# The first heads of a fused attention, routing and feed-forward kernel: small GpSimd transfers moved back, zeros on TensorE, one head prepared a step later

## The chip, the cores and the metric

The kernel runs on 1 core of one Trainium2 chip. The metric is the device time of one execution in microseconds (us). Before the change it is 897.05 us, the median of 3 runs (896.64 to 898.61). The changed kernel is timed in the same way.

The core has TensorE (PE in the profile; its weight loads are PEld), VectorE (DVE), ScalarE (ACT), GpSimd (POOL) and SyncE (SP). SP and POOL issue the transfers (DMA) of this kernel, each from a queue of its own that is worked off in order.

## The reference, cut to what matters

Three stages follow each other. Only the first is touched by the change.

```python
scores = scale * np.matmul(q, k.transpose(0, 1, 3, 2))      # 4 x 8 heads, 576 rows, 64 wide
cum = np.cumsum(np.maximum(s, 0.0), axis=-1)
bias = -(cum[:, :, :, None] - cum[:, :, None, :])
scores = np.where(causal, -1e9, scores + np.minimum(bias, 0.0))
attn = softmax(scores)                                      # with 1e-9 in the sum
x = np.matmul(attn, v)                                      # heads side by side: 2304 x 512
x = moe(x, w_gate, w1, w2)          # each token goes to one of 8 experts, 288 tokens each
out = gelu_like(x @ w_in) @ w_out   # h / (1 + exp(-1.702 h)) between the two products
```

## The kernel before, in words

**Heads and steps.** The 32 heads of attention run as a software pipeline. One step of the list `SEQ` works on several heads at once: in step i, TensorE computes the scores of head i+1 (`S`, in three units 2, 1, 0), transposes the probabilities of heads i and i-1 (`T`) and multiplies older ones with v (`A`); VectorE does row maxima (`M`) and the low parts (`L`); ScalarE does the exponentials (`X`) and the high parts (`H`). In the order of a step, `S2` of the next head comes early, then `T3` and `A0` of the head before, then `S1`, `T0`, `T1`, `A1`, `S0`. The score tiles have few buffers: `S2` of a head reuses the buffer that `X2` of the head before has read.

**Preparing a head.** For each head, q and k are written as a high and a low part into two stacked operands, `X0[i]` (first 128 rows of the contraction) and `X1[i]` (68 rows). `X1` is one tile `x1` with `HS = 6` slots. Its rows 64 to 67 hold ones, minus ones and the running sums of s: first ones and minus ones are put there for all slots, then each head's sums are written over half of them by two transfers of 4.5 KB from the DRAM tile `c_rows` (`part("c", i)`, L110 and L111). `scores` issues for each unit the products with `X0` (x = 0) and then those with `X1` (x = 1).

- Heads 0 and 1 are prepared by ScalarE and VectorE (L113 to L121), with loads per head (L310) and their sums written straight from SBUF (L327, L328).
- Heads 2 and 3: ScalarE does three operations (`Aq` L113, `Ak` L115, `Aq1` L117), GpSimd two (`kl` L106, `ql` L104).
- Heads from 4 on: ScalarE does one (`Aq`), GpSimd three (`k` L102, `kl`, `ql`), and SP copies q's high part (`q1`, L108, a transfer of 145 KB).

`load(j)` (L79) brings q and k of the pair of heads 2j and 2j+1 in four transfers of 290 KB; `load_v(j)` (L85) brings v of a pair in two (280 and 10 KB); `split_v` (L91, L92, on GpSimd) makes its high and low parts.

**What sets the order.** The first block, from the first load to `load(3)`, is ordered by hand on all five queues: SP and POOL issue there in the order of the text. From the steps on only PE, ACT and DVE are ordered by hand; the order on SP and POOL comes from the planner. `HIGH` tells in which step `high(i)` of a head is issued: `HIGH.get(j, j - 5)`. For heads from 4 on `prep(i)` (v, the sums' transfers, `k`, `kl`) goes at the head of that same step. An odd head's `high` also issues the next load, `load((i + 5) // 2)`, which needs the buffer of the pair two before it.

**GpSimd's transfers at the start.** `rest` (L318) copies the ones and minus ones of slot 0 to slots 1 to 5: 4 partitions, issued at once after the constants. Two more (L341) bring the gate's weights into `fold`, in pieces of 32 bytes.

**Zeros on TensorE.** Later in the kernel, `pulse` (L691) multiplies a tile of zeros to keep TensorE busy between the routing's small products. Before the change nothing of the kind stands at the start.

Of the kernel before, what the change touches and what calls it, by code (L numbers as in the profile page):

```python
# [8 lines left out]
F32 = mybir.dt.float32  # L9
# [9 lines left out]
BF = mybir.dt.bfloat16  # L19
# [9 lines left out]
P, T = 116, 5  # L29
# [13 lines left out]
def f32(ap):  # L43
    return ap.bitcast(F32)
# [3 lines left out]
def tile_kernel(ctx, tc, qt, kt, v, s, w_gate, w1, w2, w_in, w_out, out):  # L48
    nc = tc.nc
    V, A, G, PE, SY = nc.vector, nc.scalar, nc.gpsimd, nc.tensor, nc.sync  # L50
    keep = ctx.enter_context(tc.tile_pool(name="keep", bufs=1))
# [10 lines left out]
    ps = actx.enter_context(tc.tile_pool(name="ps", bufs=2, space=PSUM))  # L62
# [4 lines left out]
    st = {}  # L67
# [5 lines left out]
    def load(j):  # L73

        b, h = divmod(2 * j, H)
        t = att.tile([128, 2, 2, SP], F32, name="raw", bufs=3)
        for n, src in enumerate((qt, kt)):
            for r in (slice(0, 64), slice(64, 128)):
                SY.dma_start(t[r, n], src[b, h:h + 2].rearrange("h d s -> d h s"))  # L79
        st["raw", j] = t  # L80

    def load_v(j):
        t = att.tile([P, 2, T, D], F32, name="vraw", bufs=3)
        for r in (slice(0, 112), slice(112, P)):
            SY.dma_start(t[r].rearrange("p g t d -> p (g t d)"), v[j, r])  # L85
        st["v", j] = t
# [12 lines left out]
    def part(what, i):  # L99
        t, x0, x1 = st["raw", i // 2][:, :, i % 2], X0[i % HS], X1[i % HS]  # L100
        if what == "k":
            return G.tensor_scalar(x0[:, 1], t[:, 1], sc[:, 1:2], None, op0=OP.mult)  # L102
        if what == "ql":
            return G.tensor_tensor(x0[UP, 0], t[UP, 0], f32(x0[UP, 0]), op=OP.subtract)  # L104
        if what == "kl":
            return G.tensor_tensor(x1[LO, 1], t[LO, 1], f32(x0[LO, 1]), op=OP.subtract)  # L106
        if what == "q1":
            return SY.dma_start(f32(x1[LO, 0]), f32(x0[LO, 0]))  # L108
        if what == "c":
            SY.dma_start(f32(x1[66:68, 0]), c_rows[i])  # L110
            return SY.dma_start(f32(x1[64:66, 1]), c_rows[i])  # L111
        if what == "Aq":
            return A.activation(x0[:, 0], t[:, 0], AF.Copy, scale=sc[:, 0:1])  # L113
        if what == "Ak":
            return A.activation(x0[:, 1], t[:, 1], AF.Copy, scale=sc[:, 1:2])  # L115
        if what == "Aq1":
            return A.activation(x1[LO, 0], t[LO, 0], AF.Copy, scale=0.125)  # L117
        if what == "Vql":
            return V.tensor_tensor(x0[UP, 0], t[UP, 0], f32(x0[UP, 0]), op=OP.subtract)
        if what == "Vkl":  # L120
            return V.tensor_tensor(x1[LO, 1], t[LO, 1], f32(x0[LO, 1]), op=OP.subtract)  # L121

    def prep(i, c=True):
        if i % 2 == 0 and i // 2 + 1 < NH // 2:
            load_v(i // 2 + 1)
        if c:
            part("c", i)
        if i >= 4:
            part("k", i)
            part("kl", i)  # L130
        if i % 2 == 0:
            split_v(i // 2 - 1)
        elif i == NH - 1:
            split_v(i // 2)

    def high(i):

        if 2 <= i < 4:
            for what in ("Aq", "Ak", "Aq1"):
                part(what, i)  # L140
            part("kl", i)
        elif i >= 4:
            part("Aq", i)
            part("q1", i)
        if i >= 2:
            st["prep", i] = part("ql", i)
        if i % 2 and (i + 5) // 2 < NH // 2:
            load((i + 5) // 2)
# [8 lines left out]
    def scores(i, u, xs=(0, 1), mask=True):  # L157
        X = X0[i % HS], X1[i % HS][:68]
        if ("sc", i, u) not in st:
            st["sc", i, u] = ps.tile([P, 1024 if u == 0 else 512], F32, name="s4" if u == 0 else "sc", bufs=1 if u == 0 else 2)  # L160
        p = st["sc", i, u]
        banks = [c0 // 512 for _, c0, _, _ in UNITS[u]]
        for m, (t, c0, k0, w) in enumerate(UNITS[u]):
            for x in xs:
                PE.matmul(p[:, c0:c0 + w], X[x][:, 0, t * P:(t + 1) * P], X[x][:, 1, k0:k0 + w],  # L165
                          start=x == 0 and banks[m] not in banks[:m],
                          stop=x == 1 and (k0 + w < (t + 1) * P if mask else banks[m] not in banks[m + 1:]))
        if not mask:
            return
        d, n = DIAG[u], len(DIAG[u])  # L170
        step = d[-1] - d[0] if n > 1 else P
        o = p[:, d[0]:d[0] + n * step].rearrange("p (a c) -> p a c", a=n)[:, :, :P] if d[0] + n * step <= p.shape[1] \
            else p[:, d[0] + P - step:d[0] + P - step + n * step].rearrange("p (a c) -> p a c", a=n)[:, :, step - P:]
        PE.matmul(o, identb[:P, :P], maskb[:P, None, :P].to_broadcast([P, n, P]), start=False, stop=1 in xs)  # L174
# [113 lines left out]
    x1 = consts.tile([128, HS, 2, SP], F32R, name="x1")  # L288
# [10 lines left out]
    wg = w_gate.rearrange("(h d) e -> d h e", d=D)  # L299
    sums = consts.tile([P, 5, T, 2], F32, name="sums")  # L300
    warm = consts.tile([1, 2], F32, name="warm")
    G.memset(warm, 0.0)
    with (tc.manual_schedule(engines={PE.engine, A.engine, V.engine, SY.engine, G.engine})):

        SY.dma_start(cs, s)
        first_raw = st["raw", 0] = att.tile([128, 2, 2, SP], F32, name="raw", bufs=3)
        for i in range(2):
            for n, src in ((0, qt), (1, kt)):
                for r in (LO, UP):
                    SY.dma_start(first_raw[r, n, i], src[0, i])  # L310
        A.activation(warm, warm, AF.Exp)
        G.memset(f32(x1[64:68, 0, 0]), 1.0)
        V.memset(f32(x1[64:68, 0, 1]), -1.0)
        G.memset(sc, 1.0)
        G.memset(sc[LO, 0:1], 0.125)
        G.memset(sc[UP, 1:2], 0.125)
        rest = f32(x1[64:68, 1:]).rearrange("p i n s -> p i (n s)")
        G.dma_start(rest, f32(x1[64:68, 0]).rearrange("p n s -> p (n s)")[:, None, :].to_broadcast(list(rest.shape)))  # L318
        G.memset(sums, 1e-9)

        V.tensor_scalar(cs, cs, 0.0, None, op0=OP.max)
        V.tensor_tensor_scan(c_sum, cs, cs, 0.0, op0=OP.add, op1=OP.max)
        A.activation(chl[:, 0], c_sum, AF.Copy)
        V.tensor_scalar(identf, jp, 0.0, None, op0=OP.is_equal)
        V.tensor_tensor(chl[:, 1], c_sum, f32(chl[:, 0]), op=OP.subtract)
        for h in range(2):
            SY.dma_start(f32(X1[h][66:68, 0]), f32(chl[h:h + 1]))  # L327
            SY.dma_start(f32(X1[h][64:66, 1]), f32(chl[h:h + 1]))  # L328
        SY.dma_start(c_rows, f32(chl))
        for what in ("Aq", "Ak", "Aq1", "Vql", "Vkl"):  # L330
            part(what, 0)
        V.tensor_scalar(identb, jp, 0.0, None, op0=OP.is_equal)
        V.tensor_scalar(maskb, jp, 0.0, -1e9, op0=OP.is_gt, op1=OP.mult)
        for what in ("Aq", "Ak", "Aq1", "Vql", "Vkl"):
            st["prep", 1] = part(what, 1)
        V.tensor_tensor(fold[:, :, :D], identf[:, None, :D].to_broadcast([128, H, D]),
                        identf[:, None, D:].to_broadcast([128, H, D]), op=OP.add)
        load(1)
        load_v(0)
        for g in range(2):  # L340
            G.dma_start(fold[g * D:(g + 1) * D, :, D:], wg)  # L341
        part("c", 2)
        prep(3)
        load(2)
        load_v(1)
        prep(2, False)
        load(3)

    FN = dict(S=lambda i, u: scores(i, u) if i else scores(0, u, (1,), False), M=row_max, X=exps, T=transp, H=p_hi, L=p_lo, A=av, O=av_out, N=norm, R=recip, F=fin, G=fin_out)

    HIGH = {2: 0, 3: 0, 4: 1, 5: 1, 6: 2, 7: 2}

    def steps(i0, i1):
        for i in range(i0, i1):
            new = [j for j in range(NH) if HIGH.get(j, j - 5) == i]
            for j in new:
                if j >= 4:
                    prep(j)
            for f, lag, *a in SEQ:
                if f == "Q":  # L360
                    for j in new:
                        high(j)
                else:
                    on(FN[f], i - lag, *a)
# [2 lines left out]
    att_engines.enter_context(tc.manual_schedule(engines={PE.engine, A.engine, V.engine}))  # L367
    for u in (2, 1, 0):
        scores(0, u, (0,))
    steps(-3, 14)  # L370

    zeros = keep.tile([128, 128], BF, name="zeros")
    late = ExitStack()
    late.enter_context(tc.issue_after(st["prep", 17].ins))
    G.memset(zeros, 0.0)
    jrow = rt.tile([128, 128], F32, name="jrow")
    G.iota(jrow, pattern=[[1, 128]], base=0, channel_multiplier=0, allow_small_or_imprecise_dtypes=True)
    pcol = rt.tile([128, 1], F32, name="pcol")
# [782 lines left out]
    with tc.manual_schedule(engines={PE.engine, A.engine, V.engine}):  # L1161
        for q in range(NQ):
            c, p = divmod(q, PP)
# [54 lines left out]
            n, src = (4, g[:, :4]) if last else (7, g[:, 1:])  # L1218
# [52 lines left out]
```

## Time and profile before

| | |
|---|---|
| median of 3 runs | 897.05 us (896.64 to 898.61) |
| profiled execution, its own time | 896.56 us |
| span of that execution, first to last instruction | 894.8 us |
| what lies around the span | 1.76 us |
| mean granted TensorE clock | 0.973 of full speed |
| PE busy | 840.4 us, 94% of the span, 6853 matmuls |
| DVE, ACT, POOL busy | 723.6, 509.0, 276.8 us |
| moved by DMA | 124.38 MB |
| PE's busy tenths in the first five of 40 slices | 4, 7, 9, 9, 9 |

The page cuts the span in 40 slices of 22.4 us. In the first two, PE is busy for less than 8 tenths, in the following ones for 9 and more. Everything that the change edits is issued in the first 60 us. A busy PE need not be at full speed: the granted clock of a stretch says which of two levels, 1.2 and 2.4 GHz, it had (0.50 and 1.00 in the profile). Where a wait is for several things, the profile names the one that came last by its own account.

### The profile page before, as it was taken

Reading aid. Unit: us, or ns where it says so; the run is one execution under the profiler, and the core shown is the slowest. Engines: PE = TensorE matmul, PEld = TensorE weight load, DVE = VectorE, ACT = ScalarE, POOL = GpSimd, SP = SyncE. Lnnn points to the kernel's source line nnn. Section 1 sums busy time; section 2 is a strip of 40 time slices with the busy share of each in tenths; the row PEclk is TensorE's granted clock in tenths of the full one; section 3 lists DMA queues with packets and bytes.
Section 4 is the critical chain, followed back from the end, with each engine's and each line's share of the span. In section 5 each row is a group of like instructions: output and inputs, shape, how many; then the busy total and the mean of one; then the engine's idle time right before and its main releaser. Section 6 shows DMA issues by size and latency. Waiting matters only on the chain.

```text
span 894.8 us, 18574 instructions
## 1 busy us (share of the span) xinstructions
PE 840.4 (94%) x6853; PEld 821.0 (92%) x6853; DVE 723.6 (81%) x1683; ACT 509.0 (57%) x1141; POOL 276.8 (31%) x263
## 2 busy tenths in 40 slices
PE   4799999999669899999999999999999999999996
PEld 3699999999538899999999999999999999999996
DVE  4678889888777689999897798899978977777775
ACT  5889998997534557666664343434335434444442
POOL 2999999983242111021100011111010111111112
PEclk9899999999769999999999999999999999999999
DMA  6886558620346689888874333323256111111101
GB/s 160 193 199 167 149 136 217 156 75 6 123 146 104 226 243 280 258 270 248 258 236 181 99 118 101 118 83 111 73 189 222 56 49 48 48 48 49 48 24 49
DMA packets 88391, 124.38 MB, mean 139 GB/s; under 512 B 10541, under 2 KB 56769, under 8 KB 87781
## 3 DMA queue, kind: packets, MB, share of 16 engines
q1 hardware_dynamic: 85156, 113.55, 43.4%
q0 software_dynamic: 3136, 9.57, 3.7%
q8 instruction: 57, 0.93, 0.4%
q14 instruction: 42, 0.34, 0.1%
HBM read 96.61 MB, written 22.21 MB: 133 GB/s over the span
## 4 chain that ended last, share of the span: by engine, by line
PE 48%; DVE 12%; issue 4%; ACT 3%; DMA 2%; POOL 1%; SPq 0%; POOLq 0%; DVEq 0%; ACTq 0%
PE h L1013 13%; PE y L1045 11%; PE y L908 11%; PE h L898 11%; DVE g L1031 3%; DVE gT L1223 3%; ACT gT L1219 2%; DVE g L1025 2%; DVE part L1076 1%; PE h L873 1%; DVE tmp L1076 1%; DMA wi_dram<-wist 1%; DVE u L814 1%; DMA raw<-in_moe_w_in_dram 1%; DVE yc L941 1%
## 5 line engine op out<-in xcount | busy, mean ns | idle before, releaser
L1013 PE MATMUL h<-yc,win 128*128 128x256 f32 x1728 | 218.6, 283 | 0.0
L1013 PEld LDWEIGHTS h<-yc,win 128*128 128x128 f32 x1728 | 212.4, 192 | 0.0
L1045 PE MATMUL y<-wout,gT 128*128 128x256 f32 x1491 | 189.6, 282 | 7.0 <-DVE part L1076 3.9
L1045 PEld LDWEIGHTS y<-wout,gT 128*128 128x128 f32 x1491 | 180.9, 189 | 9.7 <-issue 4.2
L1219 ACT ACTIVATE gT<-g 128x896 fp32r<-128x896 f32 x72 | 68.4, 950 | 140.5 <-DVE g L1031 139.6
L908 PE MATMUL y<-hT,w2s 128*128 128x288 f32 x768 | 115.8, 299 | 0.0
L898 PE MATMUL h<-xT,w1s 128*128 128x288 f32 (+2 forms) x776 | 114.2, 295 | 0.0
L908 PEld LDWEIGHTS y<-hT,w2s 128*128 128x128 f32 x768 | 107.4, 191 | 0.0
L898 PEld LDWEIGHTS h<-xT,w1s 128*128 128x128 f32 x776 | 106.5, 188 | 0.1
L217 DVE TENSOR_TENSOR phl<-pt,phl 116x464 fp32r<-116x464 f32 (+1 forms) x128 | 76.2, 599 | 28.0 <-ACT phl L212 27.9
L1223 DVE TENSOR_TENSOR gT<-g,gT 128x896 fp32r<-128x896 f32 x72 | 78.9, 1096 | 16.4 <-ACT gT L1219 16.3
L1031 DVE TENSOR_TENSOR g<-g 128x128 f32<-128x128 f32 x284 | 75.2, 306 | 4.9
L228 PE MATMUL pt<-phl,vhl 116*128 116x232 f32 (+2 forms) x512 | 75.7, 291 | 2.4 <-POOL vhl L92 2.1
L212 ACT ACTIVATE phl<-pt 116x464 fp32r<-116x464 f32 (+1 forms) x128 | 69.2, 541 | 12.4 <-PE pt L206 12.1
L670 POOL DMA_INDIRECT xg<-x_rows,idx x24 | 29.3, 1222 | 141.2 <-PE h L873 134.8
L228 PEld LDWEIGHTS pt<-phl,vhl 116*128 116x128 f32 x512 | 66.4, 194 | 4.0 <-POOL vhl L92 2.8
L1080 POOL DMA_INDIRECT out_dram<-part,oids x18 | 22.2, 1231 | 150.5 <-DVE part L1076 150.5
L1020 ACT ACTIVATE sg<-h 128x256 f32<-128x256 f32 x84 | 32.1, 384 | 64.1 <-PE h L1013 63.5
L206 PE MATMUL pt<-identf,pr 116*116 116x116 f32 x480 | 66.7, 271 | 0.9 <-DVE phl L217 0.7
L1021 DVE TENSOR_TENSOR g<-h,sg 128x256 f32<-128x256 f32 x84 | 35.5, 423 | 32.9 <-ACT sg L1020 32.3
L165 PE MATMUL sc<-x 128*116 128x348 f32 (+3 forms) x192 | 44.8, 342 | 16.0 <-ACT x L115 10.4
L206 PEld LDWEIGHTS pt<-identf,pr 116*116 116x116 f32 x480 | 52.5, 143 | 4.4 <-PE sc L174 1.0
(199 smaller groups left out, 1433.6 us busy)
## 6 DMA issues: line engine op xcount, KB each, us to landing
wraw<-in_moe_w_dram SPq DMA_DIRECT2D x60, 512.0 KB
yraw<-y_dram SPq DMA_DIRECT2D x18, 512.0 KB
raw<-in_qt_dram SPq DMA_DIRECT2D x30, 290.0 KB
raw<-in_kt_dram SPq DMA_DIRECT2D x30, 290.0 KB
raw<-in_moe_w_in_dram SPq DMA_DIRECT2D x32, 256.0 KB
raw<-in_moe_w_out_dram SPq DMA_DIRECT2D x32, 256.0 KB
y_dram<-yt SPq DMA_DIRECT2D x8, 576.0 KB
vraw<-in_v_dram SPq DMA_DIRECT2D x16, 280.0 KB
```

What stands on the lines that cost most here:

```text
L165: PE.matmul(p[:, c0:c0 + w], X[x][:, 0, t * P:(t + 1) * P], X[x][:, 1, k0:k0 + w], start=x == 0 and banks[m] not in banks[:m], stop=x == 1 ...
L206: PE.transpose(p[:, w - P:w], pr[:, place(t, c):place(t, c + 1)], identf[:P, :P])
L212: A.activation(hl[:, 0], p, AF.Copy)
L217: st["lo", i] = V.tensor_tensor(hl[:, 1], st["pt", i, g], f32(hl[:, 0]), op=OP.subtract)
L228: PE.matmul(p[:, t0 * P:(t0 + n) * P], vhl[:, hh, c].rearrange("p a d -> p (a d)"), st["phl", i, g][:, x, col:col + n * P], start=x == 0 a ...
L898: PE.matmul(p[:, o], w[:, a, k, c], x[:, b, k, o], start=n == 0 and (e, m) != (0, 0), stop=n == len(steps) - 1)
L908: PE.matmul(py[d], w[:, a, m % 2, d * 128:(d + 1) * 128], h[:, b], start=m == 0 and n == 0, stop=m == 7 and n == 2)
L1013: PE.matmul(h, w[:, a, k], yc[c][:, b, k], start=n == 0 and (both is None or half == 0), stop=n == 11 and (both is None or half == 1))
L1031: V.tensor_tensor(g[:, o], g[:, a], g[:, b], op=op)
L1045: PE.matmul(acc[b][:, o * 256:o * 256 + 256], t[:, j, x], wout[:, p, i, y], start=p == 0 and n == 0 and b not in banks[:m], stop=end and n ...
L1219: A.activation(t[:, 0, :n], src, AF.Copy)
L1223: V.tensor_tensor(t[:, 1, :n], src, f32(t[:, 0, :n]), op=OP.subtract)
```

## The change

- `rest` moves from the constants to behind `load_v(0)`. In front of it POOL now does a `tensor_copy` of one number out of v's first tile, and a `memset` that sets that number's place back. `rest` covers slots 2 to 5 only; the two memsets of slot 0 (L312, L313) now cover slots 0 and 1. The two `fold` transfers stay behind it.
- `idle(n)` is new: n products of zeros, 128 x 512, into a PSUM tile of the transposes' kind. `idle(12)` is PE's first work; `idle(6)` comes after the x = 0 products of head 0's scores and before the x = 1 products. The tile `zeros` is made at the start instead of later.
- `HIGH` puts heads 3, 5 and 7 one step later each: 3 in step 1, 5 in step 2, 7 in step 3. With them go their loads, `load(4)`, `load(5)` and `load(6)`, and for 5 and 7 the work of `prep`.

```diff
+    zeros = keep.tile([128, 128], BF, name="zeros")
+    G.memset(zeros, 0.0)
     G.memset(warm, 0.0)
+    def idle(n):
+        p = ps.tile([P, 512], F32, name="pt", bufs=4)
+        for i in range(n):
+            PE.matmul(p, zeros[:, :P], zeros[:, None, :].to_broadcast([128, 4, 128]), start=i == 0, stop=i == n - 1)
...
         A.activation(warm, warm, AF.Exp)
-        G.memset(f32(x1[64:68, 0, 0]), 1.0)
-        V.memset(f32(x1[64:68, 0, 1]), -1.0)
+        idle(12)
+        G.memset(f32(x1[64:68, 0:2, 0]), 1.0)
+        V.memset(f32(x1[64:68, 0:2, 1]), -1.0)
...
-        rest = f32(x1[64:68, 1:]).rearrange("p i n s -> p i (n s)")
-        G.dma_start(rest, f32(x1[64:68, 0]).rearrange("p n s -> p (n s)")[:, None, :].to_broadcast(list(rest.shape)))
...
         load(1)
         load_v(0)
+        G.tensor_copy(sums[:1, 0, 0, 1:2], st["v", 0][:1, 1, 0, :1])
+        G.memset(sums[:1, 0, 0, 1:2], 1e-9)
+        rest = f32(x1[64:68, 2:]).rearrange("p i n s -> p i (n s)")
+        G.dma_start(rest, f32(x1[64:68, 0]).rearrange("p n s -> p (n s)")[:, None, :].to_broadcast(list(rest.shape)))
         for g in range(2):
             G.dma_start(fold[g * D:(g + 1) * D, :, D:], wg)
         part("c", 2)
...
-    HIGH = {2: 0, 3: 0, 4: 1, 5: 1, 6: 2, 7: 2}
+    HIGH = {2: 0, 3: 1, 4: 1, 5: 2, 6: 2, 7: 3}
...
     for u in (2, 1, 0):
         scores(0, u, (0,))
+    idle(6)
     steps(-3, 14)
-    zeros = keep.tile([128, 128], BF, name="zeros")
     late = ExitStack()
     late.enter_context(tc.issue_after(st["prep", 17].ins))
-    G.memset(zeros, 0.0)
```

## Rows read from the trace of the kernel before

**Rows 1.** TensorE's instructions in order of time: first scores of steps 1 to 5.

```profile
24.06 0.71 PE L165 MATMUL sc<-x 128*116 128x348 f32 x4 [2.53 <-POOL x L106]
...
27.67 1.79 PE L228 MATMUL pt<-phl,vhl 116*128 116x348 f32 x6 [2.13 <-POOL vhl L92]
...
33.87 0.71 PE L165 MATMUL sc<-x 128*116 128x348 f32 x4
...
40.14 0.39 PE L165 MATMUL sc<-x 128*116 128x348 f32 x1
42.89 0.55 PE L165 MATMUL sc<-x 68*116 68x348 f32 x3 [2.36 <-DMA x<-c_rows]
...
50.94 0.72 PE L165 MATMUL sc<-x 128*116 128x348 f32 x4
...
57.22 0.71 PE L165 MATMUL sc<-x 128*116 128x348 f32 x4
```

**Rows 2.** Busy time by stretch: us, length, PE, PEld, DVE, ACT, POOL, clock, DMA share, GB/s.

```profile
6.00:7.00 1.00, 0.00 (x0) 0.00 (x0) 0.76 (x1) 0.00 (x0) 0.00 (x0) 1.00 0.28 35
...
25.00:31.00 6.00, 3.87 (x17) 3.26 (x16) 4.18 (x11) 4.74 (x14) 6.00 (x4) 0.50 1.04 214
32.00:45.00 13.00, 10.58 (x94) 10.04 (x94) 8.72 (x21) 9.81 (x29) 12.82 (x10) 1.00 0.79 169
...
46.00:48.00 2.00, 2.00 (x11) 1.75 (x10) 0.63 (x2) 0.92 (x5) 1.92 (x3) 0.50 0.51 121
...
50.00:60.00 10.00, 10.00 (x92) 9.89 (x91) 8.39 (x23) 9.16 (x27) 9.85 (x8) 1.00 0.97 234
```

**Rows 3.** ScalarE in order of time: preparing heads 0, 2 and 3.

```profile
9.56 0.78 ACT L115 ACTIVATE x<-raw,sc 128x580 fp32r<-128x580 f32 x1 [3.69 <-DMA raw<-in_kt_dram]
...
19.83 0.78 ACT L115 ACTIVATE x<-raw,sc 128x580 fp32r<-128x580 f32 x1 [1.79 <-DMA raw<-in_kt_dram]
...
21.09 0.76 ACT L113 ACTIVATE x<-raw,sc 128x580 fp32r<-128x580 f32 x1
...
23.00 0.53 ACT L192 ACTIVATE pr<-sc,nm 116x348 f32<-116x348 f32 x1
```

**Rows 4.** SP's queue in order of time: issues of transfers, neighbours merged.

```profile
2.44 1.24 SPq L310 DMA_DIRECT2D raw<-in_kt_dram  x2
3.71 3.85 SPq L310 DMA_DIRECT2D raw<-in_qt_dram  x2
...
9.06 0.74 SPq L327 DMA_DIRECT2D x<-xs  x1
...
12.14 1.41 SPq L79 DMA_DIRECT2D raw<-in_qt_dram  x2
...
18.47 1.89 SPq L79 DMA_DIRECT2D raw<-in_qt_dram  x2
...
33.57 0.23 SPq L110 DMA_DIRECT2D x<-c_rows  x1
...
38.80 2.55 SPq L108 DMA_DIRECT2D x<-x  x2
```

**Rows 5.** GpSimd in order of time: rest's issue, v's cast, two low parts.

```profile
2.22 0.98 POOL L318 DMA_DIRECT2D x<-x  x1
...
21.05 0.72 POOL L91 CAST vhl<-vraw 116x640 fp32r<-116x640 f32 x1 [1.46 <-DMA vraw<-in_v_dram]
...
38.82 2.79 POOL L106 TENSOR_TENSOR x<-raw,x 64x580 fp32r<-64x580 f32 x2
```

**Rows 6.** DMA issues of the first 60 us: KB each, median us to landing.

```profile
x<-x POOLq DMA_DIRECT2D x1, 90.6 KB, 6.7
```

**Rows 7.** The chain that ended last, at the routing's gather: start, us.

```profile
266.59 3.72 DMA xg<-x_rows,idx
```

**Rows 8.** VectorE in order of time: its wait for the first load.

```profile
2.64 0.45 DVE L321 TENSOR_SCALAR xs<-xs 32x580 f32<-32x580 f32 x1 [1.19 <-DMA xs<-in_s_dram]
```

**Rows 9.** TensorE in order of time: zeros of the routing, after idle time.

```profile
259.60 3.19 PE L691 MATMUL warm<-zeros 128*128 128x512 bf16 x7
```

## The prediction

> **What bounds the kernel now.** Read first the page's busy shares in 40 slices: PE is short of work in the first two slices and near the end of attention, nearly nowhere else, and all that the change edits is issued in the first 60 us. So the question is what the first steps cost. Read second PE's own order of time and look only at where each step's first scores stand [rows 1]. From 50.94 to 57.22 a step takes 6.28 us with PE busy throughout [rows 1, 2]; that is the price of a step that lacks nothing. Step 1 (24.06 to 33.87) takes 9.81, step 2 (33.87 to 40.14) 6.27, step 3 (40.14 to 50.94) 10.80. Step 1 has lost 3.5 us and step 3 4.5. From step 4 on PE is full until the routing, so a shift of step 4's start, now at 50.94, should reach the end one for one. I forecast that one number.
>
> Third, the clock of these stretches [rows 2]: 0.50 from 25 to 31 and from 46 to 48, that is 1.2 GHz of 2.4. Each follows an idle PE by some us: the wait in front of 24.06 (2.53) and the one in front of 42.89 (2.36) [rows 1]. A wait of this length costs itself and then some us at the lower level.
>
> Fourth, who ends the waits. In step 0, ScalarE stands until 19.83 for k of heads 2 and 3 [rows 3], then does two operations for head 2 and three for head 3, and only at 23.00 the exponential that frees the buffer for the scores of 24.06; the profile names GpSimd, which came about as late. In step 1, PE waits 2.13 for v's low part [rows 1], since v's cast could only begin at 21.05, when v had landed [rows 5]. In step 3 it waits for a transfer into x. The queue shows which: the copy of q's high part for head 4 is issued at 38.80 [rows 4], behind two more loads of pairs, with issues that stand for earlier transfers to land from 33.57 on.
>
> **Part 1: GpSimd's transfers leave the start.** rest is issued at 2.22 [rows 5] and needs 6.7 us to land [rows 6]. Meanwhile the DMA engines are at 0.28 (6 to 7 us) though ScalarE waits until 9.56 for k of head 0 [rows 2, 3]: about 4.5 of 16 engines work, which fits 4 partitions of rest on a few engines that all loads need too. SP is held as well: two issues take 3.85 us where the two before took 1.24 [rows 4]. With rest and fold gone I expect each issue at 0.62. SP's 8 loads then end at 2.44 + 6 x 0.62 = 6.2 instead of 8.85, and the rest of its list moves forward by 2.6 to 2.9: load(1) from 12.14 to 9.3 [rows 4]. Taking 2.9: k of heads 2 and 3 lands at 16.9 instead of 19.83, v at 18.1 instead of 21.05 [rows 3, 5]. Bounds: 0 if the stall was not rest's, 3.5 if the loads also land faster.
>
> **Part 2: they come back behind v.** GpSimd now stands until v has landed (18.1); the copy and the memset take some 0.2 (between nothing and the cast's 0.72 [rows 5]); then it issues rest. When rest lands is not in the trace. The bounds: 6.7, rest's own time among the loads [rows 6], and 1.9, the first load of s (issued at 0.72, used at 2.64 [rows 8]). The nearest row is a GpSimd transfer on an otherwise quiet DMA, the routing's gather, 3.72 [rows 7], and SP will be quiet here. I take it: rest lands at 18.3 + 3.7 = 22.0.
>
> The Trainium skill ("DMA: Bandwidth & Descriptors", section on the anatomy of one SWDGE transfer) fits a transfer issued by GpSimd as 2.0 us plus its bytes over 436 GB/s; for these 74 KB that is an estimate of 2.2, and by it all that follows would come 1.5 us sooner. The two rows on GpSimd's transfers here, 3.72 and 6.7, are both above it, so it is not used.
>
> Behind that landing two queues stand. On SP the sums of head 2 (c) write into rows that rest writes, so they wait, and behind them the sums of head 3, load(2), v of the next two pairs and load(3). On GpSimd, fold's two issues (1.46 by the row of before, which is not on the path), the cast, and head 2's low part wait for v; they are through at about 23, before PE asks. The sums are issued at 22.0 and 22.3 (0.23 each [rows 4]) and take the 1.9 of a small load to land: PE gets the x = 1 scores of head 2 at 24.2, against 24.06 before. So step 0 gains nothing: what part 1 saves is spent on waiting for rest. ScalarE is through with head 2 by 19.4 and idles.
>
> **Part 3: zeros.** One product of zeros takes 3.19 / 7 = 0.46 us at the lower clock [rows 9], half of that at the upper. idle(12) takes at most 5.5 us from 1.3 on and ends at about 6.8, when k of head 0 has come: hidden. idle(6) puts 1.4 to 2.7 us in front of head 0's x = 1 products; its cover is the wait for rest, since ScalarE's exponentials of head 1 would end at 19.4 and PE waits until 24.2. Without that cover the 1.4 to 2.7 would be on the path. What the zeros give: a higher clock for heads 0 and 1, which then wait anyway. PE idles for about 5 us before 24.2, twice the idles that preceded the lower clock, so step 1 begins at 1.2 GHz as before. I cost part 3 at 0.
>
> **Part 4: head 3 a step later.** Three ScalarE operations (21.09 to 23.00, 1.91 us [rows 3]) leave step 0 and enter step 1, head 5's one leaves step 1 for step 2, and so on; by step 3 the sum is the same. GpSimd's two operations for head 3 move too, and load(4), load(5), load(6).
>
> *Step 1.* Gone: the wait for v's low part, 2.13. Added on ScalarE: 1.91 less the one operation of head 5 (0.76); but the exponentials of head 1, which stood in step 1 before, are done while PE waits for rest. I take 9.81 - 2.13 + 0.3 = 8.0, between 6.28 (nothing lost) and 9.81. Step 2 begins at 32.2 and step 3 at 38.5 (6.27, as before).
>
> *Step 3.* It needs c and q1 of head 4. Before, load(4) stood ahead of them on SP; now load(4) belongs to step 1 and needs the buffer of heads 2 and 3, which GpSimd frees late, so I expect q1 ahead of it. What is still ahead: load(2), load(3) and three loads of v, 3.2 MB. Before, v's arrival at 21.05 freed the DMA engines for load(2) and q1 landed at 42.86, with 4.4 MB in between: 203 GB/s. Now load(2) is issued at 23.1, behind four transfers of sums, and data flow some 1.5 later: 24.6 + 3.2 MB / 203 = 40.4. PE waits 1.9 us instead of 2.36 and scores head 4 at 40.4 instead of 42.89.
>
> *To step 4.* Before, 42.89 to 50.94 is 8.05; with a clock that holds it is 6.28 - 0.39 = 5.9. The wait of 1.9 is shorter than both that were followed by the lower clock, so I take that it holds, and 0.8 for head 5's copy, which now lands behind load(4) (between 0 and the 2.1 of a clock that falls). Step 4 begins at 40.4 + 5.9 + 0.8 = 47.1 instead of 50.94: 3.8 us sooner.
>
> **Sum.** Part 1 -2.9, all spent in part 2 (+3.0); part 3 0; step 1 -1.8; step 3 -2.1: -3.8, against the profiled execution's 896.56 us (894.8 span and 1.76 around it): 892.8. The median of the runs shown is 0.49 above that execution; the forecast is 893.2.
>
> **The rivals.** "Measurable" is 0.2%, 1.8 us here.
>
> *A, load(4) ahead of q1 (slower).* If the planner still puts load(4) before head 4's copy, 1.19 MB at 214 GB/s [rows 2] come in between: q1 lands at 40.4 + 5.5 = 45.9, the wait becomes 7 us, the clock falls as before, and step 4 begins at 45.9 + 8.05 = 53.9: 3.0 slower, 900.0. It decides from the point at which q1 lands after 42.9. For it: before, every load went in the text's order up to load(4). Against: load(4)'s buffer is free later now. 0.15.
>
> *B, rest lands late.* With its 6.7 everything from head 2's scores on moves by 3.0: q1 at 43.4, clock falls, step 4 at 51.4, +0.5: 897.5. For it: the only row of rest itself. Against: no load runs beside it now. 0.10. The Trainium skill speaks for B in "DMA: Bandwidth & Descriptors", rules for kernel authors: issue a transfer early and wait late, so that its fixed cost is hidden. Here the change does the reverse, and the rows agree that it was hidden before in step 0, at the cost of the stall of part 1.
>
> *C, GpSimd late.* Before, head 4's low part of k ran only at 38.82 [rows 5], after higher heads' work, and GpSimd was busy without a break. If the planner's order leaves it as far back, counted from k of head 4, it ends near 43 and step 3 loses what it lost before; only step 1's gain is left and is eaten there: 0 to -1, 896.5. 0.14.
>
> *D, all goes through.* rest lands in 2.2 and the wait of step 3 is under 1 us: step 4 at 43.5 to 44.5, -7: 890. 0.10.
>
> *E, part 1 gives nothing* (the stall has another cause): v at 21, rest at 25, like B. 0.03.
>
> The forecast has 0.48 with its own range of 891 to 895.2. Faster: 0.48 + D 0.10 + a part of C and B 0.06 = 0.64. Slower: A 0.15 and 0.03 of B and E = 0.18. The same: 0.18. The range leaves A's far half and the outer part of D out: 889.5 to 898.5.
>
> **What would show it.** Right: SP's eight loads issued at about 0.6 each, k of head 0 at 6 instead of 9.56; v at 18; SP standing until 22; head 2's scores at 24 with a low clock behind them; no wait for v's low part; step 3's wait under 2 us; step 4 before 48. Wrong: a wait of PE in step 3 that begins before 40 and ends after 43; L79's load(4) before L108 on SP; the sums of head 2 issued after 24; heads 0 and 1 so late, by the zeros, that ScalarE is not through with head 2 at 24.

## The result, and the profile after

The changed kernel takes 905.6 us, the median of 4 runs (904.94 to 908.95), against 896.9 for the kernel before beside it: a ratio of 1.0103, with a 95% interval of 1.0077 to 1.0129. It is some 9 us slower where 3.8 us faster was forecast, and outside the range. The profiled execution took 904.94 us with a span of 903.1.

TensorE in order of time, kernel after. The number in front of the engine is the instruction's length; the bracket is the idle time before it and what ended it.

```profile
26.62 0.90 PE L165 MATMUL sc<-x 68*116 68x348 f32 x3 [6.52 <-DMA x<-c_rows]
...
34.12 0.72 PE L165 MATMUL sc<-x 128*116 128x348 f32 x4
...
42.70 0.62 PE L165 MATMUL sc<-x 128*116 128x348 f32 x1
49.08 0.90 PE L165 MATMUL sc<-x 68*116 68x348 f32 x3 [5.76 <-DMA x<-c_rows]
...
54.85 1.79 PE L228 MATMUL pt<-phl,vhl 116*128 116x348 f32 x6 [2.24 <-POOL vhl L92]
...
61.22 0.72 PE L165 MATMUL sc<-x 128*116 128x348 f32 x4
...
67.50 0.71 PE L165 MATMUL sc<-x 128*116 128x348 f32 x4
```

Read it against [rows 1]. Step 1 starts with a wait of 6.52 us and computes head 2's second half of scores at 26.62. Step 2 begins at 34.12, only 0.25 later than before. Then step 3 loses: it waits 5.76 us for head 4's operands and 2.24 for v's low half, and step 4 begins at 61.22 instead of 50.94, 10.3 us late. From there a step takes 6.28 us as before.

SP's queue in order of time, kernel after.

```profile
3.71 1.24 SPq L319 DMA_DIRECT2D raw<-in_qt_dram  x2
...
9.43 1.42 SPq L79 DMA_DIRECT2D raw<-in_qt_dram  x2
...
18.48 0.23 SPq L110 DMA_DIRECT2D x<-c_rows  x1
18.75 0.25 SPq L111 DMA_DIRECT2D x<-c_rows  x1
24.70 0.22 SPq L110 DMA_DIRECT2D x<-c_rows  x1
...
25.86 1.25 SPq L79 DMA_DIRECT2D raw<-in_qt_dram  x2
...
38.20 1.83 SPq L79 DMA_DIRECT2D raw<-in_qt_dram  x2
40.80 2.06 SPq L79 DMA_DIRECT2D raw<-in_kt_dram  x2
43.79 0.52 SPq L108 DMA_DIRECT2D x<-x  x1
```

The two issues that took 3.85 us take 1.24, and load(1) goes out at 9.43 instead of 12.14 [rows 4]. But SP issues nothing from 19.0 to 24.70. The view of waits names what it stands for:

```profile
SPq L110 <- DMA x<-x: 5.6, 1, 5.6
```

That is one wait of 5.6 us of the sums (L110) for the transfer of ones that GpSimd issues behind v. Ahead of it SP had already stood for 5.3 us, up to 18.48, in front of another pair of sums that the planner put there; the second wait covers this one, since the sums of head 2 could not leave before 24.70 in any case. load(2) stands behind these sums and leaves at 25.86, against 18.47 before. Head 4's copy of q leaves at 43.79, behind load(4), against 38.80 before.

GpSimd in order of time, and the group of DMA issues with its landing time, kernel after.

```profile
18.09 0.18 POOL L349 COPY sums<-vraw 1x1 f32<-1x1 f32 x1 [0.21 <-DMA vraw<-in_v_dram]
18.25 1.41 POOL L106 TENSOR_TENSOR x<-raw,x 64x580 fp32r<-64x580 f32 x1
19.61 0.09 POOL L350 MEMSET sums<- 1x1 f32 x1
19.66 0.84 POOL L352 DMA_DIRECT2D x<-x  x1
...
42.43 3.44 POOL L102 TENSOR_SCALAR x<-raw,sc 128x580 fp32r<-128x580 f32 x2 [3.46 <-DVE phl L217]
45.85 2.76 POOL L106 TENSOR_TENSOR x<-raw,x 64x580 fp32r<-64x580 f32 x2
...
53.26 1.54 POOL L92 TENSOR_TENSOR vhl<-vraw,vhl 116x640 fp32r<-116x640 f32 x1
```

```profile
x<-x POOLq DMA_DIRECT2D x1, 72.5 KB, 5.0
```

The planner has put head 2's low part of k (18.25) between the copy and the memset, so the transfer leaves at 19.66 and lands 5.0 us later. At 42.43 GpSimd waits in front of k of heads 6 and 7, and the low parts of k of heads 4 and 5 (45.85) stand behind these.

Stretches of the kernel after, columns as in [rows 2]:

```profile
20.00:25.00 5.00, 0.10 (x1) 0.00 (x0) 2.16 (x4) 2.84 (x9) 4.22 (x5) 0.64 0.20 21
25.00:31.00 6.00, 4.38 (x20) 4.16 (x21) 2.27 (x7) 2.37 (x4) 1.39 (x1) 0.50 0.65 151
...
45.00:59.00 14.00, 7.69 (x35) 7.10 (x36) 3.37 (x10) 3.69 (x11) 13.83 (x11) 0.50 0.82 188
```

The first of these stretches in the kernel before:

```profile
20.00:25.00 5.00, 2.47 (x16) 2.27 (x16) 0.57 (x2) 5.00 (x12) 3.80 (x4) 0.96 0.92 234
```

From 20 to 25 the DMA engines move 21 GB/s at a share of 0.20 where it was 234 at 0.92, and from 25 to 31 151 GB/s where it was 214 [rows 2]: the loads that could run stand in SP's queue. From 45 to 59 the granted clock is 0.50, 1.2 GHz of 2.4, behind the long wait of step 3; before, that level held from 46 to 48.

### The profile page after: what moved, and what is told of

Read it like the earlier page. It is cut to its first block, busy times and chain, and to the rows that moved or that the text cites. A ratio compares the mean times of both kernels' runs of the same rounds, so it can differ in the third digit from the quotient of the medians.

```text
span 903.1 us, 18611 instructions
## 1 busy us (share of the span) xinstructions
PE 849.9 (94%) x6871; PEld 825.8 (91%) x6871; DVE 723.4 (80%) x1683; ACT 509.0 (56%) x1141; POOL 279.2 (31%) x265
## 4 chain that ended last, share of the span: by engine, by line
PE 48%; DVE 12%; issue 4%; ACT 3%; DMA 1%; POOL 1%; SPq 0%; POOLq 0%; DVEq 0%; ACTq 0%
PE h L1025 13%; PE y L1057 11%; PE y L920 11%; PE h L910 11%; DVE g L1043 3%; DVE gT L1235 3%; ACT gT L1231 2%; DVE g L1037 2%; DVE part L1088 1%; PE h L885 1%; DVE tmp L1088 1%; DMA wi_dram<-wist 1%; DVE u L826 1%; DMA raw<-in_moe_w_in_dram 1%; DVE yc L953 1%
## 5 line engine op out<-in xcount | busy, mean ns | idle before, releaser
L184 DVE TENSOR_REDUCE nm<-sc 116x1 f32<-116x348 f32 (+2 forms) x96 | 42.6, 472 | 20.2 <-PE sc L174 17.2
```

## The experiments

Theory 1: the cost is the place of the transfer of ones. The sums of heads 2 and 3 wait in SP's queue for it, and load(2) and all behind it with them. Theory 2: head 3 and the odd heads a step later cost it, through the order of loads and copies. Theory 3: the zeros delay something. All ratios are to the kernel before on the same chip; "step 4" is where the first scores of step 4 start in the one profiled execution of each, so it is no better than one execution (that of E3 took 901.68 us, 4.7 above the median of E3).

| kernel | ratio, 95% interval | step 4 at, us |
|---|---|---|
| before | 1 | 50.94 |
| after | 1.0103 (1.0077 to 1.0129) | 61.22 |
| E1, the transfers alone moved | 1.0086 (1.0061 to 1.0112) | 58.27 |
| E2, heads later alone | 1.0030 (1.0002 to 1.0059) | 52.28 |
| E3, zeros alone | 1.0003 (0.9977 to 1.0028) | 53.24 |
| E4, after with load(2) ahead of the sums | 1.0033 (1.0014 to 1.0052) | 52.10 |
| E5, after with memsets for the transfer | 1.0052 (1.0029 to 1.0075) | 52.04 |
| E6, memsets alone | 1.0008 (0.9985 to 1.0031) | 49.86 |
| E7, E6 with zeros | 0.9989 (0.9966 to 1.0012) | 50.10 |
| E8, after with q of head 4 ahead of load(4) | 1.0119 (1.0051 to 1.0188) | 60.38 |
| E9, E6 with v's low half first | 1.0002 (0.9981 to 1.0023) | 48.61 |
| E10, E9 with zeros | 0.9985 (0.9963 to 1.0008) | 47.17 |
| E11, E9 with half the transfer | 1.0027 (1.0004 to 1.0050) | 49.30 |
| E12, E10 with low halves on VectorE | 0.9930 (0.9905 to 0.9955) | 44.83 |
| E13, E12 with heads later | 1.0001 (0.9975 to 1.0027) | 46.57 |

### One part alone: E1, E2, E3

E1, the kernel before with the transfers moved:

```diff
-        rest = f32(x1[64:68, 1:])...; G.dma_start(rest, ...)      # at the start
+        G.tensor_copy(sums[:1, 0, 0, 1:2], st["v", 0][:1, 1, 0, :1])   # behind load_v(0)
+        G.memset(sums[:1, 0, 0, 1:2], 1e-9)
+        rest = f32(x1[64:68, 2:])...; G.dma_start(rest, ...)
```

> The kernel before with the small transfers alone moved behind v(0); no zeros on TensorE, head 3 where it was. Theory 1 (the sums of heads 2 and 3 stand in SP's queue until these transfers have landed, and load(2) and all behind it with them, some 7 us): 901 to 907 us, head 2's second half of scores near 26 us, load(2) issued after 24 us. Theory 2 (head 3 and the odd heads a step later cost it): 894 to 897 us, the early start of load(1) kept.

E2:

```diff
-    HIGH = {2: 0, 3: 0, 4: 1, 5: 1, 6: 2, 7: 2}
+    HIGH = {2: 0, 3: 1, 4: 1, 5: 2, 6: 2, 7: 3}
```

> The kernel before with heads 3, 5 and 7 a step later and nothing else. Theory 1: 893 to 898 us, since load(2) keeps its place near 18.5 us, and the planner puts head 4's q ahead of load(4) in SP's queue. Theory 2: 903 to 906 us, with the steps 3 and 4 spread as in the kernel after.

E3:

```diff
         A.activation(warm, warm, AF.Exp)
+        idle(12)
...
         scores(0, u, (0,))
+    idle(6)
```

> The kernel before with the two groups of zero products alone (12 ahead of head 0, 6 ahead of head 2). Theories 1 and 2: 896 to 898 us, no change, since TensorE waits for keys there anyway. Theory 3 (the zeros delay the first scores or spend clock that step 3 lacks later): 900 us or more.

Measured: 903.48, 899.04 and 896.99 us against 895.53. E1 has nearly the whole loss by itself. TensorE and GpSimd of E1 in order of time:

```profile
26.49 0.90 PE L165 MATMUL sc<-x 68*116 68x348 f32 x3 [4.65 <-DMA x<-c_rows]
...
48.59 0.90 PE L165 MATMUL sc<-x 68*116 68x348 f32 x3 [5.70 <-DMA x<-x]
```

```profile
41.65 3.44 POOL L102 TENSOR_SCALAR x<-raw,sc 128x580 fp32r<-128x580 f32 x2 [2.05 <-DMA raw<-in_kt_dram]
45.07 1.40 POOL L106 TENSOR_TENSOR x<-raw,x 64x580 fp32r<-64x580 f32 x1
```

The same two waits stand there as in the kernel after, and here the profile names what GpSimd stood for at 41.65: k of load(3). So the late load(2) and load(3) reach step 3 by two ways, through SP's queue and through GpSimd's. E2 costs some 2.7 us by its ratio and lies outside both ranges that were expected: it is more than theory 1 allowed and a third of what theory 2 needed. Its interval just leaves out no change. In its trace TensorE waits 2.10 and 0.84 us ahead of head 3's scores for the two low halves that GpSimd now makes later, and step 4 begins 1.3 us late; a wait of 1.57 us for GpSimd follows at 142.28. Theory 3 falls: E3 makes no difference.

### The wait or the order: E4, E5, E8

E4, the kernel after with the sums of heads 2 and 3 behind load(2):

```diff
-        part("c", 2)
-        prep(3)
         load(2)
         load_v(1)
         prep(2, False)
+        part("c", 2)
+        prep(3)
         load(3)
```

> The kernel after with load(2) and v(1) issued ahead of the sums of heads 2 and 3 on SP; the small transfers stay behind v(0). Theory 1: load(2) near 19 us, no standstill of SP's queue behind them, 892 to 899 us. Theory 2: no gain, 903 to 907 us. If only the order of load(4) and head 4's q costs it (here q stands ahead again): 898 to 901 us with head 2's second half of scores still near 26.6 us or later.

E5, the kernel after with memsets for the transfer:

```diff
+        G.memset(f32(x1[64:68, 2:, 0]), 1.0)      # at the start, behind the memset of sums
+        G.memset(f32(x1[64:68, 2:, 1]), -1.0)
...
-        rest = f32(x1[64:68, 2:])...; G.dma_start(rest, ...)
```

> The kernel after with the small transfer behind v(0) replaced by two GpSimd memsets of the same rows at the start, so that no transfer has to land before the sums of heads 2 and 3. Theory 1 (they stand in SP's queue for that landing): load(2) issued near 18 us or before, 893 to 899 us, 7 to 12 below the kernel after; what is left over the kernel before is head 3's new place, 1.003 as measured alone. Theory 2 (the order of the heads costs it): 900 to 906 us.

E8, the kernel after with load(4) emitted behind head 4's copy, and the next two likewise:

```diff
+        if i in (3, 5, 7):
+            return
+        if i in (4, 6, 8):
+            load((i + 4) // 2)
         if i % 2 and (i + 5) // 2 < NH // 2:
             load((i + 5) // 2)
```

> The kernel after with load(4), load(5) and load(6) issued behind the copies of heads 4, 6 and 8, so that head 4's q stands ahead of load(4) as the prediction had it; the small transfer stays. Theory 1: load(2) still near 26 us and head 2's second half near 26.6 us; head 4's q lands some 5 us earlier, and step 4 comes 2 to 5 us earlier: 900 to 904 us. If the order of load(4) and head 4's q is all that went wrong: 893 to 897 us.

Measured: 898.97 us against 895.53, 901.35 and 906.65 against 896.26. E4 keeps the transfer and all the rest of the change, and its sums are even later, yet two thirds of the loss are gone. SP of E4, and TensorE:

```profile
13.20 1.25 SPq L79 DMA_DIRECT2D raw<-in_qt_dram  x2
...
28.62 0.22 SPq L110 DMA_DIRECT2D x<-c_rows  x1
```

```profile
30.42 0.90 PE L165 MATMUL sc<-x 68*116 68x348 f32 x3 [9.98 <-DMA x<-c_rows]
...
44.04 0.71 PE L165 MATMUL sc<-x 128*116 128x348 f32 x4
```

load(2) leaves at 13.20. Head 2's second half comes 3.8 us later than in the kernel after (30.42), and step 3 still begins without a wait at 44.04, and step 4 at 52.10. So what costs is not that head 2 is late but that the loads behind its sums are. load(3) still stands behind the sums in E4 and leaves at 29.84, hardly before its 30.24 in the kernel after, so the loads that count are load(2) and those of v next to it. What is left of the loss, 1.0033, is about what the later heads cost alone (E2, 1.0030). But 898.97 also lies in the range that was expected if the order of load(4) and head 4's q were all, and in E4 q is ahead (35.21, load(4) at 38.85); that rival is left to E8.

E8 keeps the late load(2) and puts q ahead. The ratio is 1.0119; the interval, from four executions, leaves room for a gain of some 5 us over the kernel after, but not for the 893 to 897 us that were expected if the order were all. Theory 1's own 900 to 904 us, with step 4 earlier by 2 to 5 us, were missed too: step 4 is 0.8 us earlier. SP, GpSimd and TensorE of E8:

```profile
38.48 0.53 SPq L108 DMA_DIRECT2D x<-x  x1
39.72 1.84 SPq L79 DMA_DIRECT2D raw<-in_qt_dram  x2
```

```profile
42.63 3.44 POOL L102 TENSOR_SCALAR x<-raw,sc 128x580 fp32r<-128x580 f32 x2 [3.61 <-DVE phl L221]
46.05 2.77 POOL L106 TENSOR_TENSOR x<-raw,x 64x580 fp32r<-64x580 f32 x2
```

```profile
47.50 0.93 PE L169 MATMUL sc<-x 68*116 68x348 f32 x3 [3.95 <-POOL x L106]
```

q leaves 5.3 us earlier than in the kernel after, and step 3 waits for GpSimd's low part of k instead, until 47.50. Either of the two queues is enough for most of that wait.

E5 takes the transfer away and gains no more than E4: 901.35 us lies in theory 2's range (900 to 906) and not in theory 1's. load(2) leaves at 15.83 there, but TensorE waits 11.21 us, until 31.83, for the low half of v(0), which the planner put behind k of heads 4 and 5, and 2.31 us for GpSimd at 142.96. So E5 exchanges one wait for others, and the cost of the transfer's wait is read from E1 and E4 and not from E5.

### Where the gain of the start goes: E6, E7, E9, E10, E11

E6 is E5 without zeros and with the heads where they were; E7 is E6 with the zeros. E6 against E5:

```diff
-        idle(12)
...
-    idle(6)
...
-    HIGH = {2: 0, 3: 1, 4: 1, 5: 2, 6: 2, 7: 3}
+    HIGH = {2: 0, 3: 0, 4: 1, 5: 1, 6: 2, 7: 2}
```

> The kernel before with the small transfers at the start replaced by memsets, the fold's rows moved behind v(0), no zeros, head 3 where it was. Theory 1: the start gives its 2.9 us and nothing takes them back but the loads' later waits: 888 to 895 us. Rival (the start's gain is worth nothing, since step 4 waits for load(4) and head 4's q all the same): 895 to 897 us.

> As the one with the memsets and all else of the change, but with head 3 and the odd heads where they were before. Theory 1: as the memsets alone, 888 to 895 us, since the zeros change nothing; Theory 2: below the one with head 3 a step later by 5 us or more. The new places alone gave 1.003, so 2 to 4 us below it are expected.

Measured: 897.57 and 894.72 us against 896.26. Neither can be told from the kernel before, though the sums of heads 2 and 3 are issued from 13.25 on and load(2) at 16.12 in E6. The expectation of 888 to 895 was wrong for E6 and just held for E7. E7 is 6.6 us below E5, which is the sign that was named for theory 2: beside memsets the later heads cost more than alone. TensorE of E6:

```profile
21.62 1.19 PE L165 MATMUL sc<-x 128*116 128x348 f32 x4 [3.08 <-issue]
...
30.81 1.79 PE L228 MATMUL pt<-phl,vhl 116*128 116x348 f32 x6 [7.22 <-POOL vhl L92]
...
37.29 0.72 PE L165 MATMUL sc<-x 128*116 128x348 f32 x4
```

Head 2's scores come 2.4 us earlier than in [rows 1], and then TensorE waits 7.22 us for the low half of v(0): the planner put it behind the low parts of head 3, k of heads 4 and 5 and the cast of v(1), which waits for a load. E9 pins it behind its cast (the edit is shortened here):

```diff
-            G.tensor_copy(hl[:, :, :, 0], raw)                     # cast of v(1), v(2)
+            with tc.issue_after(low_half_of_v0): G.tensor_copy(hl[:, :, :, 0], raw)
...
-        if what == "k": ...                                        # and "ql", "kl"
+        if what in ("k", "ql", "kl") and i in (3, 4, 5): ...   # issued after low_half_of_v0
```

> The kernel with memsets in the small transfers' place, no zeros and head 3 where it was, and v(0)'s low half on GpSimd put right behind its cast, ahead of heads 3 to 5 and of v(1)'s cast. Theory 1 with its addition (there the gain of the start went into the 7.2 us that TensorE waited for v(0)'s low half, because the planner had put it behind other work): head 0's first product with v near 25 us instead of 30.8, step 2 near 31.5, 890 to 894 us. Rival (the loads bound these steps, whatever GpSimd does): the wait comes back ahead of step 3 or 4, 895 to 898 us.

> The same with the zeros on TensorE. All theories: within 2 us of the one without them, since each stands in a wait for keys; if the zeros hold the higher clock through the first heads for good, 2 to 4 us faster.

E10 puts back `idle(12)` and `idle(6)`. E11 is E9 with the transfer kept for heads 4 and 5 and memsets for heads 2 and 3:

```diff
-        G.memset(f32(x1[64:68, 2:, 0]), 1.0)
-        G.memset(f32(x1[64:68, 2:, 1]), -1.0)
+        G.memset(f32(x1[64:68, 2:4, 0]), 1.0)
+        G.memset(f32(x1[64:68, 2:4, 1]), -1.0)
...
+        rest = f32(x1[64:68, 4:])...; G.dma_start(rest, ...)
```

> The same as the first of these three, but with the small transfer behind v(0) kept for heads 4 and 5 alone (half its bytes), and memsets for heads 2 and 3, so that the sums of heads 2 and 3 don't wait for it. Theory 1 (the wait in SP's queue costs, not the traffic): as the first of these within 2 us. Rival (the transfer itself holds up the loads beside it): 3 to 6 us slower than the first.

Measured: 896.81, 895.30 and 899.69 us against 896.75. TensorE of E9:

```profile
23.74 1.79 PE L237 MATMUL pt<-phl,vhl 116*128 116x348 f32 x6 [0.56 <-POOL vhl L95]
...
39.33 0.93 PE L174 MATMUL sc<-x 68*116 68x348 f32 x3 [2.03 <-POOL x L115]
...
138.57 0.57 PE L174 MATMUL sc<-x 68*116 68x348 f32 x3 [1.54 <-POOL x L115]
```

The product with v comes at 23.74, as expected, and step 4 at 48.61, 2.3 us earlier than before. But the wait comes back twice as a wait for GpSimd's low part of k, ahead of step 3 and again at 138.57, and the whole gains nothing: the rival's 895 to 898 us came true, but with GpSimd as the bound and not the loads, since GpSimd works without a break from 18.09 to 40.77. E10's zeros give 1.5 us by the medians, those of E7 2.9 against E6, and the intervals overlap in both pairs: a gain by the zeros is not shown. E11 is 2.9 us above E9 with overlapping intervals, and its step 4 is 0.7 later. Whether the transfer's traffic costs a little beside its wait stays open; it is not where the 9 us are.

### GpSimd relieved: E12, E13

Open after these runs was how the loss divides, since the heads' later place cost 2.7 us alone and more beside memsets (E5 against E7, 6.6 us). E12 is E10 with the low halves of heads 2 and 3 on VectorE and head 4's q ahead of load(4) as in E8; E13 differs from it in `HIGH` alone, as in E2.

```diff
-            part("kl", i)                    # heads 2 and 3, GpSimd
-            st["prep", i] = part("ql", i)
+            st["prep", i] = part("Vql", i)   # VectorE
+            part("Vkl", i)
```

> Memsets in the small transfers' place, zeros, v(0)'s low half first on GpSimd, and the low halves of heads 2 and 3 (q and k, four subtractions of 1.4 us) on VectorE, which idles there from 15 to 22 us; head 4's q ahead of load(4); head 3 where it was. If GpSimd's queue is what bounds the steps once the start is earlier: the wait ahead of step 3 and the one near 138 us shrink, 889 to 893 us. If the loads bound them: 894 to 897 us, as without it.

> The same with head 3 and the odd heads a step later, as in the kernel after. If head 3's later place costs only because its low halves come late on GpSimd (the 2.1 and 0.8 us that TensorE waited for them ahead of step 2): within 2 us of the one with head 3 where it was, or faster. If the later place costs by itself (order of loads and copies behind it): 3 to 7 us slower than that one.

Measured: 891.29 and 898.94 us against 898.64. E12 is faster than the kernel before, 0.9930 (0.9905 to 0.9955), and so than the kernel after. It differs from E10 by two things, the low halves and the place of head 4's q, and these were not taken apart. TensorE of E12, then of E13:

```profile
37.06 0.72 PE L179 MATMUL sc<-x 128*116 128x348 f32 x4
...
40.38 1.03 PE L242 MATMUL pt<-phl,vhl 116*128 116x348 f32 x6 [1.22 <-POOL vhl L95]
...
44.83 0.71 PE L179 MATMUL sc<-x 128*116 128x348 f32 x4
```

```profile
137.27 0.58 PE L179 MATMUL sc<-x 68*116 68x348 f32 x3 [2.27 <-POOL x L115]
...
207.25 0.51 PE L220 MATMUL pt<-identf,pr 116*116 116x116 f32 x3 [2.22 <-DVE phl L231]
```

E12's step 3 begins without a wait at 37.06, step 4 at 44.83 (6.1 us before [rows 1]), and no wait for GpSimd is left near 138 us. E13 is 7.7 us slower by the medians, so the later place costs even with these low halves off GpSimd. Only 1.7 us of it are there at step 4 (46.57). The rest appears later, in waits that E12 does not have, such as the two shown, and behind both the granted clock falls: to 0.59 from 137 to 143 and to 0.73 from 207 to 213, where E12 has 1.00. The wait for GpSimd near 140 us also stands in E2 and E5, but with the heads in their old place, too (E7, 1.52 us at 140.03); why the later place costs more was not traced further. The wait at 207.25 is behind VectorE, which stands for a small store and reload of the routing (4.37 us in E13, 2.04 in E12, 2.27 in the kernel before). The profiled executions of E3 and E7 stand as long there (4.14 and 4.64) and took 4 to 5 us more than the medians of their kernels, so this wait can be one of the single execution and not of the later place.

## Why the prediction was wrong

**Part 1 was right as a mechanism.** SP's eight loads took 0.62 each, load(1) left at 9.43 (9.3 forecast), and v was there at 18.09 (18.1 forecast). What the forecast did not see is that this is worth nothing until everything behind it moves too: E6 has this gain without any wait for the transfer, and is not measurably faster. The runs moved `rest` and the `fold` transfers together, so which of the two had held the loads is not shown.

**Part 2 failed in two terms.** The transfer left at 19.66, not 18.3, because the planner set head 2's low part of k into the part that I had read as fixed by hand, and it landed after 5.0 us, not 3.7. The sums went out at 24.70 instead of 22.0, and load(2), forecast at 23.1, left at 25.86, 7.4 us later than before, with idle DMA engines ahead of it. The price in part 2, "what part 1 saves is spent on waiting for rest", counts head 2's scores alone. These are nearly free (E4: 3.8 us later, and faster by two thirds of the loss). The wait in front of the loads in SP's queue is what E1 charges with 7.7 us of the 9; E6, which has no such wait, is at 1.0008.

**Part 3 held:** the zeros cost nothing that these runs can tell (E3).

**Part 4, step 1, was near** (7.5 us against 8.0). **Step 3 failed, and here the forecast gain became a loss.** It carried the delay of load(2), but through SP's queue alone, and set against it that q of head 4 would stand ahead of load(4): head 4's scores at 40.4. With load(2) at its measured 25.86 the same sum gives 43.2; the scores came at 49.08, and the other 5.9 us are what the sum did not have. "I expect q1 ahead of it" was wrong; load(4) left at 38.20 and q at 43.79. But rival A, which names this, is not the cause by itself either: with q ahead the loss stays (E8). Rival C, GpSimd late, happened as well: the low part of k ended near 47, behind k of heads 6 and 7, which waited for load(3) by the row of E1. A and C were priced as alternatives at 3.0 and about 0; they share one origin, the late load(2), and came together.

**Rival B had the right cause and the wrong price,** 0.5 us instead of 9. Its condition, a landing at 25.0, is nearly what happened (sums at 24.70). It let all move by 3.0 us, as one piece, with 8.05 us from head 4's scores to step 4 as before. What it lacked is that the loads' delay reaches GpSimd too, and that this last piece took 12.14 us, with 2.24 of waiting for v's low half in it and the clock at 0.50 until 59. On B the prediction cited the Trainium skill, "DMA: Bandwidth & Descriptors", rules for kernel authors, to issue early and wait late. The runs agree with it: the transfers issued late, with the wait right behind them, cost 7.7 us by themselves (E1).

**"One for one" was near for this change and is no rule.** The 10.3 us at step 4 are 10.2 at the routing's first product (244.12 against 233.97) and 8.4 at the end of the profiled executions. But E9 and E13 begin step 4 by 2.3 and 4.4 us earlier and end level with the kernel before. The forecast counted on TensorE alone being full from step 4 on, and named a busy GpSimd only for step 3 (rival C); GpSimd was full after it as well. Stretches of the kernel before:

```profile
40.00:60.00 20.00, 17.58 (x141) 16.79 (x140) 14.10 (x36) 15.14 (x44) 19.70 (x15) 0.91 0.79 188
60.00:80.00 20.00, 20.00 (x181) 19.55 (x179) 16.99 (x42) 18.82 (x55) 19.40 (x15) 1.00 0.53 129
```

GpSimd is busy for 19.4 to 19.7 us of every 20. That this is what takes an earlier start back is argued, from the waits for GpSimd in E9 and E13 and from E12, which has none near 140 us. It is not shown as the whole: E9 still has 1.3 of its 2.3 us at the routing's first product (232.66), and one of E13's two waits is behind VectorE.

**The moved heads** cost 2.7 us alone (E2) where the forecast had a gain in step 1. In the kernel after, the wait of 2.24 us for v(1)'s low half seems to be theirs: E1, which differs by them and the zeros, has none there, and its step 4 is 2.95 us earlier.

## What to carry to other kernels

Before moving a transfer to a place where something must wait for it, list what stands behind the waiter in its queue: here the late sums were nearly free and the loads behind them cost some 8 us. When two engines in order both stand for the same late load, repairing one order shows only the other. And when an earlier start gains nothing, look for the engine that is full behind the one that is the bound; here four subtractions moved from GpSimd to a VectorE that had nothing to do, together with an earlier copy of head 4's q, took the ratio from 0.9985 (E10) to 0.9930 (E12).

## What the runs showed of the hardware

The small transfer of GpSimd is not priced by its bytes. It landed after 6.7 us with 90.6 KB among the first loads [rows 6] and after 5.0 with 72.5 KB on a nearly idle DMA; in E4, where loads ran beside it, the sums that wait for it left 7.9 us after its issue (20.73 to 28.62), and in E11 half the bytes took longer than the whole in the kernel after:

```profile
x<-x POOLq DMA_DIRECT2D x1, 36.2 KB, 7.2
```

The Trainium skill ("DMA: Bandwidth & Descriptors", section on the anatomy of one SWDGE transfer) gives 2.0 us plus the bytes over 436 GB/s, an estimate of 2.2 for the 72.5 KB; every one of these rows is above twice that.

GpSimd's copy of one element took 0.18 us in the kernel after and 0.76 in E12, and its cast of v 1.26 instead of 0.77, each beside a subtraction of VectorE. GpSimd of E12, then VectorE:

```profile
18.28 0.76 POOL L365 COPY sums<-vraw 1x1 f32<-1x1 f32 x1 [10.84 <-DMA vraw<-in_v_dram]
...
20.78 1.26 POOL L94 CAST vhl<-vraw 116x640 fp32r<-116x640 f32 x1
```

```profile
18.24 0.76 DVE L130 TENSOR_TENSOR x<-raw,x 64x580 fp32r<-64x580 f32 x1 [0.77 <-ACT x L124]
...
20.71 0.75 DVE L130 TENSOR_TENSOR x<-raw,x 64x580 fp32r<-64x580 f32 x1
```

The copy ends within 0.04 us of the subtraction. The Trainium skill ("SBUF — State Buffer", terms) says that the two engines share a pair of ports which one instruction holds to its end while the other waits; these rows agree.
